# Fewer steps of the weights' sums in tile 0's output stage, their rounding copies one step behind, the second batch normalised earlier

## The chip, the core and the metric

The kernel runs on one core of one Trainium2 chip. The metric is the device time of one execution in microseconds, as the median of several executions. A core has five engines that matter here: TensorE (PE, its weight loads PEld), VectorE (DVE), ScalarE (ACT), GpSimd (POOL) and the queue that issues transfers (SP). Each takes its own instructions in the order of its queue. An instruction whose input is not there holds up all behind it on that engine.

## The reference

```python
# attention: 8 batches, 8 heads, 576 positions, 64 wide; window of 64 positions back
scores = np.matmul(q, k.transpose(0, 1, 3, 2)) / np.sqrt(64)
scores = np.where((rel >= 0) & (rel < 64), scores, -1e9)
attn = softmax(scores)                                # + 1e-9 in the sum
x = np.matmul(attn, v)  # to 4608 tokens x 512
# gated feed-forward layer, d_ff 1536
rms = np.sqrt(np.mean(x * x, axis=-1, keepdims=True) + 1e-06)
xn = x / rms * rms_g
g = xn @ w_gate
out = (g * sigmoid(g) * (xn @ w_val)) @ w_out
```

All in float32. The kernel does the large products with pairs of float16 tiles (a rounded value and the rest), three matmuls for each product.

## The kernel before, in words

The 4608 tokens are worked through in nine tiles of 512, the attention in eight batches of 576 tokens, four pairs of heads each. A tile needs the normalised output of the batches that it overlaps: tile 1 takes the last 64 tokens of batch 0 and the first 448 of batch 1. Attention of later batches runs among the matmuls of earlier tiles.

**Half-steps.** A tile has 32 half-steps: 24 of its input stage (`expert_in`: gate and value products, banks `pg` and `pv`, six blocks of 256 columns of d_ff, two accumulations of each kind in a block) and 8 of its output stage (`expert_out`: four chunks `po` of 128 tokens, 36 matmuls each; `store` drains a chunk with ScalarE into `ot`, L1219, and SP writes it out). Tile 0 spans half-steps 0 to 32, its output stage 24 to 32, tile 1 32 to 64, tile 2 64 to 96. All other work is entered in a plan with a half-step as its due time (`at_step`). Some is placed in slots, a finer count of the matmul groups (`at_slot`); `advance` issues what is due as the matmul loop passes.

**Order.** Up to the second block of tile 1 (`ORDERED = (1, 1)`) the order of the text is only a priority: a planner with its own simulated times picks what is ready for each engine. From that block on, PE, DVE, ACT and POOL keep the written order (`in_written_order`). SP's queue stays with the planner.

**Banks.** Three accumulation banks (`mo`) are shared by `pg`, `pv` and `po`; one bank (`mi`) is shared by the totals (`tot`, L756) and both broadcasts (`rb`, L835) of a batch's normalisation. Eight buffers of 2 KB (`t2k`) are shared by `th`, `ot`, `hl`, `blk` and others.

**The weights' sums.** From tile 3 on the input products use a scheme with seven products in place of eight, which needs sums of blocks of the weights. `prepare(c, step)` makes them, eight steps for each of six column blocks c: a step adds two halves of a block (`whole_block`, L1061), or combines two sums (L1096, L1101, L1104, L1109). Four of the eight steps end in `out`: ScalarE rounds the sum to float16 (`hl`, L1071), VectorE subtracts to get the rest (L1074), and two transfers write both to `sevens` in DRAM (L1076). Step 0 also writes twelve blocks of the weights as they are (L1091). `PREP` gives two windows of half-steps with a number of steps in each. `load_sevens` (L1119) reads the sums back over the old weights, at half-steps 72, 80 and 88 for the first three column blocks.

**Normalisation of batch 1.** `attention_events(1, ...)` enters scores at the eight half-steps of `S1`, transposes `LK1` later, products with the values `LV1` later, query and key loads `LQ1` earlier. The two numbers behind these are the half-steps of the two pieces: `roots` one half-step ahead of the first (squares summed into `ssq`, totals, then eleven small instructions on VectorE, L774 and L811), then for each piece a broadcast on TensorE, four scalings on VectorE (L865), four copies on ScalarE (L869) and four subtractions on POOL (L871).

**Around it.** Pairs of batch 2 are scored in visits at half-steps 24.5 and 29.5. For each, POOL then does 16 moves (L381) and VectorE three transposes (L386, L388, `turn`). The output weights are split at half-step 23 (`out_split`, L245 on ScalarE, L246 on VectorE).

Of the kernel before, what the change touches and what calls it, by code (L numbers as in the profile page):

```python
# [2 lines left out]
def E(n, d):  # L3
    return CFG.get(n, d)
# [39 lines left out]
MOVES = (8.7, 7, 4.5, 4)  # L44
FIRST7 = 3
ORDERED = (1, 1)
PREP = ((26, 32, 24), (34, 84, 25))
MASK_AT, MASK_BY, WEIGH = 1, 1, 1
MOVE_AT, MOVE_BY, TURN_AT = 11.3, 0.8, -4
NORM_AT, NORM_BY, NORM_GAP = 5, 0.75, 2  # L50
# [1 line left out]
GATE, HH_7, HH_8 = 0, 1, 1  # L52
ST = 2 * NBLK * P - D
NRB = 2
S1, LK1, LV1, LQ1 = [-2, 1, 3, 6, 10, 12.5, 15.5, 19], 2.5, 6, 7
LN2_16 = 16 * math.log(2.0)
MASKED = -3.0e38
QK_SCALE = 1.0 / math.sqrt(D)
# [4 lines left out]
def tile_window_attention_moe(  # L63
# [10 lines left out]
    nc = tc.nc  # L74
# [60 lines left out]
    for rows, cols, own in (  # L135
# [7 lines left out]
        part = mask[rows, cols]  # L143
# [487 lines left out]
    def attention_events(b, start, pace, tags):  # L631

        load_queries, load_keys, score, to_keys, values, roots, normal, moved, turned, products, drain, norm = attention(b)
        lk, lv, lq, n0, n1 = tags
        events = []
        if b < NRB:
            events = [(n0 - 1, roots), (n0, partial(normal, 0)), (n1, partial(normal, 1))]
        else:
            s0 = slot_at(visit_at(NPAIR * b + 5))
            for k, part in enumerate(normalise_all(b, norm)):  # L640
                at_slot(s0 + NORM_AT + NORM_BY * k + (NORM_GAP if k > 2 else 0), part)
        for hp in range(NPAIR):
            if b >= TB:
                n = NPAIR * b + hp
                i0 = visit_at(n) - half_steps * (b - 1)
                events.append((i0 - 7, partial(load_queries, hp)))
                events.append((i0 - 7, partial(load_keys, hp)))
                s0 = slot_at(visit_at(n))
                for k in range(16):
                    when = MOVE_AT + MOVE_BY * k if n >= RUSH else MOVE_AT - 4.7 + 0.5 * k  # L650
                    at_slot(s0 + when, partial(moved, hp, k // 4, k % 4))
                for k in range(3):
                    at_slot(slot_at(visit_at(n + 2)) + TURN_AT - 2 * (RUSH <= n < 16) + k, partial(turned, hp, k))
                visits[n] = partial(products, hp), partial(values, hp), partial(drain, hp)
                continue
            i0 = start[2 * hp]
            events.append((i0 - lq, partial(load_queries, hp)))
            events.append((i0 - lq, partial(load_keys, hp)))
            for g in range(2):
                i = start[2 * hp + g]  # L660
                events.append((i + lv, partial(values, hp, g)))
                events.append((i + lk, partial(to_keys, hp, g)))
                events.append((i, partial(score, hp, g)))
        return events
# [4 lines left out]
    def slot_at(h):  # L669

        t, r = divmod(h, half_steps)
        per = 4 * NF if t < FIRST7 else 7 * NC
        first = t * (4 * NF + NC * TT // P) - max(0, t - FIRST7) * (4 * NF - 7 * NC)
        return first + (r * per / in_phase if r < in_phase else per + (r - in_phase) * NC / 2)
# [10 lines left out]
    def at_slot(s, part):  # L685
        at_step(step_at(s) + 1e-6, part)
# [7 lines left out]
    def visit_at(n):  # L694

        n -= NPAIR * TB
        return VISITS[n] if n < 4 else VISITS[4] + 8 * (n - 4)
# [175 lines left out]
    def normalise_all(b, norm):  # L873
        return LazyParts(b, norm).parts()
# [176 lines left out]
    unfinished = []  # L1051

    def prepare(c, step):

        w = [wt[(2 * c + i) % (2 * NC)].rearrange("p a (k f) -> p a k f", k=NKD) for i in range(2)]
        s0, s1 = sums

        def whole_block(out, f, d):
            for i in range(2):
                hi, lo = (w[i][:, j, 2 * d : 2 * d + 2, f * P : (f + 1) * P] for j in range(2))  # L1060
                nc.vector.tensor_tensor(out[:, i], hi, lo, ALU.add)  # L1061

        def block(f, d):
            t = wk.tile([P, TT], F32, tag="t2k", name=f"blk_{c}_{step}", bufs=T2K)
            kept_block["b"] = t.rearrange("p (w k f) -> p w k f", w=2, k=2)
            whole_block(kept_block["b"], f, d)

        def out(src, o):
            src = src.rearrange("p w k f -> p (w k f)")
            hl = wk.tile([P, 2, TT], F16, tag="t2k", name=f"hl_{c}_{step}", bufs=T2K)  # L1070
            nc.scalar.copy(hl[:, 0], src)  # L1071

            def rest():
                nc.vector.tensor_tensor(hl[:, 1], src, hl[:, 0], ALU.subtract)  # L1074
                for j in range(2):
                    nc.sync.dma_start(  # L1076
                        out=sevens[c][:, o, :, j].rearrange("p w k f -> p w (k f)"),
                        in_=hl[:, j].rearrange("p (w n) -> p w n", w=2),
                    )

            unfinished.append(rest)

        if unfinished:
            unfinished.pop()()
        if c == NC:
            return
        if step == 0:
            for i in range(2):
                for o, k, f in ((0, 0, 0), (1, 2, 0), (6, 2, 1)):
                    for j in range(2):  # L1090
                        nc.sync.dma_start(out=sevens[c][:, o, i, j], in_=w[i][:, j, k : k + 2, f * P : (f + 1) * P])  # L1091
            whole_block(s0, 1, 0)
        elif step == 1:
            whole_block(s1, 0, 0)
        elif step == 2:
            nc.vector.tensor_tensor(s1, s1, s0, ALU.subtract)  # L1096
            out(s1, 5)
        elif step == 3:
            block(1, 1)
        elif step == 4:  # L1100
            nc.vector.scalar_tensor_tensor(s0, s0, -1.0, kept_block["b"], ALU.mult, ALU.subtract)  # L1101
            out(s0, 2)
        elif step == 5:
            nc.vector.tensor_tensor(s1, s1, kept_block["b"], ALU.subtract)  # L1104
            out(s1, 3)
        elif step == 6:
            block(0, 1)
        else:
            nc.vector.tensor_tensor(s1, s1, kept_block["b"], ALU.add)  # L1109
            out(s1, 4)  # L1110
# [153 lines left out]
    def at_step(h, part):  # L1264
        plan.append((h, len(plan), part))

    HPLACE = "8fffff"
    SEQ = E("SEQ", "00 01 02 03 04 05 o0").replace(","," ").split()
    for h, part in attention_events(1, S1, 0, (LK1, LV1, LQ1, 28, 30)):
        at_step(h, part)  # L1270
    if E("S2", None) is not None:
        for h, part in attention_events(2, E("S2", 45), E("P2", 0.8), (E("LK2", 1.5), E("LV2", 2.5), E("LQ2", 4), E("N20", 60), E("N21", 62))):
# [15 lines left out]
    rest = first_batch()  # L1288
# [12 lines left out]
    def at(name, part):  # L1301
        if name not in done0:
            at_step(DW[name], part)
# [13 lines left out]
    at("O", out_split)  # L1317
    at_step(PREP[0][0], room_for_sums)
    done = 0
    for a, z, count in PREP:  # L1320
        s0, s1 = slot_at(a), slot_at(z)
        for j in range(count):
            at_slot(s0 + (s1 - s0) * j / count, partial(prepare, *divmod(done + j, 8)))
        done += count
# [77 lines left out]
```

## Time and profile before

| | |
|---|---|
| median of 3 runs | 1033.64 us (1033.34 to 1034.03) |
| profiled execution | 1035.58 us |
| its span, first to last instruction | 1033.4 us, mean granted TensorE clock 0.977 |
| PE busy | 976.0 us, 94% |
| DVE busy | 639.3 us, 62% |
| ACT busy | 508.0 us, 49% |
| POOL busy | 505.6 us, 49% |

The output stage of tile 0 begins at 188.09 us with the first `po` matmul, and tile 1's first gate matmul starts at 230.20. In the rows of the profile a group is named by line, engine, operation and tiles (`out<-in`); behind the bar stand busy time and mean duration in ns, and idle time before it with what ended it. A timeline's row is start, duration, engine, line; in brackets the idle time before it and its releaser.

### The profile page before, as it was taken

The numbers are of one execution on the slowest core, as the hardware profiler recorded it, in microseconds if no ns is written. First come the engines' busy times: TensorE is split into PE (matmuls) and PEld (weight loads), VectorE is DVE, ScalarE is ACT, GpSimd is POOL, SyncE is SP. The second block draws the span as 40 slices with busy tenths as digits, with TensorE's granted clock in tenths as the row PEclk, the third lists the DMA queues.
The fourth block names the chain that finished last, engine by engine and source line by source line (L and its number), as shares of the span: only waits on it lengthen the run. The fifth ranks groups of instructions, "written<-read, shape, count | busy, mean of one in ns | idle before, by whom it ended". The sixth has DMA issues, their size and how long they took to land.

```text
span 1033.4 us, 20843 instructions
## 1 busy us (share of the span) xinstructions
PE 976.0 (94%) x7835; PEld 632.1 (61%) x7835; DVE 639.3 (62%) x1721; ACT 508.0 (49%) x1303; POOL 505.6 (49%) x634
## 2 busy tenths in 40 slices
PE   7788989988999999999999999999999999999998
PEld 5544434543544455478747874787478848856875
DVE  5687756796658454646775767576666655532550
ACT  5556757625444444355545554565456524522540
POOL 3334524682976467536673677467646611200210
PEclk9988988899999999999999999999999999999999
DMA  7645793224223454247624762476246515632401
GB/s 281 196 134 163 218 278 78 69 80 123 74 63 91 123 147 148 74 148 220 202 85 146 223 205 81 137 231 196 81 123 188 165 40 146 195 116 89 151 1 41
DMA packets 81316, 143.43 MB, mean 139 GB/s; under 512 B 25792, under 2 KB 38336, under 8 KB 81216
## 3 DMA queue, kind: packets, MB, share of 16 engines
q1 hardware_dynamic: 80640, 140.93, 44.8%
q8 instruction: 61, 1.00, 0.4%
q10 hardware_dynamic: 576, 1.18, 0.3%
q14 instruction: 39, 0.32, 0.1%
HBM read 121.64 MB, written 20.45 MB: 137 GB/s over the span
## 4 chain that ended last, share of the span: by engine, by line
PE 66%; DVE 18%; ACT 8%; issue 3%; DMA 3%; POOL 2%; SPq 0%; ACTq 0%; DVEq 0%; POOLq 0%
PE bk L1136 18%; PE bk L960 5%; PE bk L961 5%; PE bk L962 5%; PE xp L534 4%; PE sc L399 3%; DVE th L1176 3%; PE pv L960 3%; PE pg L962 3%; PE pg L960 3%; PE pg L961 3%; PE pv L961 3%; PE pv L962 3%; ACT th L1167 3%; DVE th L1177 3%
## 5 line engine op out<-in xcount | busy, mean ns | idle before, releaser
L1136 PEld LDWEIGHTS <-wt 128*128 128x128 f16 x3024 | 294.9, 98 | 54.7 <-issue 18.0
L381 POOL TENSOR_TENSOR pm<-pm,st 32x288 f32<-32x288 f32 (+1 forms) x384 | 274.0, 713 | 95.2 <-DVE st L449 51.6
L1136 PE MATMUL bk<-xn,wt 128*128 128x256 f16 x1728 | 209.2, 272 | 11.3 <-DVE th L1177 5.3
L981 POOL TENSOR_TENSOR h<-th,h 128x512 f16<-128x512 f32 x78 | 91.5, 1173 | 198.8 <-ACT h L981 185.3
L1136 PE MATMUL bk<-wt,wt 128*128 128x256 f16 x1224 | 150.3, 273 | 0.3 <-ACT u L1156 0.3
L960 PE MATMUL bk<-wt,h 128*128 128x512 f16 (+1 forms) x300 | 111.3, 371 | 0.0
L962 PE MATMUL bk<-wt,h 128*128 128x512 f16 (+1 forms) x300 | 111.2, 371 | 0.0
L961 PE MATMUL bk<-wt,h 128*128 128x512 f16 (+1 forms) x300 | 111.2, 371 | 0.0
L415 ACT ACTIVATE pm<-pm,st 128x128 f32<-128x128 f32 (+1 forms) x216 | 83.7, 388 | 36.9 <-DVE st L412 36.3
L1167 ACT ACTIVATE th<-bk,hsc 128x256 f32<-128x256 f32 x108 | 50.8, 471 | 99.3 <-DVE bk L1197 67.1
L981 ACT CAST h<-th 128x512 f16<-128x512 f32 x94 | 57.8, 615 | 47.8 <-DVE th L1026 33.9
L1176 DVE SCALAR_TENSOR_TENSOR th<-th,bk 128x256 f32<-128x256 f32 x108 | 45.2, 419 | 54.5 <-ACT th L1167 54.1
L960 PEld LDWEIGHTS <-h 128*128 128x128 f16 x436 | 43.2, 99 | 50.9 <-issue 7.1
L962 PEld LDWEIGHTS <-h 128*128 128x128 f16 x436 | 43.0, 99 | 49.3 <-issue 1.4
L961 PEld LDWEIGHTS <-h 128*128 128x128 f16 x436 | 43.2, 99 | 45.6 <-issue 1.3
L399 PE MATMUL sc<-kv,q 64*64 64x128 f32 (+1 forms) x1056 | 56.9, 295 | 9.4 <-DMA q<-q 5.0
L1197 DVE TENSOR_TENSOR bk<-bk,s 128x512 f32<-128x512 f32 x36 | 24.9, 693 | 57.7 <-PE bk L1136 57.7
L960 PE MATMUL pv<-xn,wt 128*128 128x512 f16 x144 | 56.1, 390 | 3.9 <-ACT wt L239 2.0
L960 PE MATMUL pg<-xn,wt 128*128 128x512 f16 x144 | 55.9, 388 | 3.7 <-ACT ot L1219 3.7
L962 PE MATMUL pg<-xn,wt 128*128 128x512 f16 x144 | 55.3, 386 | 1.3 <-DVE wt L246 1.3
L961 PE MATMUL pv<-xn,wt 128*128 128x512 f16 x144 | 55.9, 388 | 0.0
L961 PE MATMUL pg<-xn,wt 128*128 128x512 f16 x144 | 55.7, 387 | 0.0
(191 smaller groups left out, 1754.9 us busy)
## 6 DMA issues: line engine op xcount, KB each, us to landing
wt<-sevens SPq DMA_DIRECT2D x108, 512.0 KB, 4.2
kv<-kv SPq DMA_DIRECT2D x28, 608.0 KB, 4.7
wt<-sevens SPq DMA_DIRECT2D x36, 256.0 KB, 3.4
q<-q SPq DMA_DIRECT2D x28, 288.0 KB, 3.0
kv<-kv SPq DMA_DIRECT2D x56, 128.0 KB, 4.7
out<-ot SPq DMA_DIRECT2D x27, 256.0 KB, 2.0
st<-w_gate SPq DMA_DIRECT2D x6, 1024.0 KB, 6.6
st<-w_val SPq DMA_DIRECT2D x6, 1024.0 KB, 6.4
```

The costliest lines, as they stand in the source:

```text
L381: nc.gpsimd.tensor_tensor(m[to, :us, fr], p[fr, :us, to], r, ALU.mult)
L399: nc.tensor.matmul(out.rearrange("p (n c) -> p n c", c=D), lhsT=qt[hd, j * D : (j + 1) * D], rhs=halves[hd, :1, :] if j == 0 else halves[h ...
L415: nc.scalar.activation(part, part, AF.Exp, bias=low, scale=-1.0, accum_out=total)
L534: nc.tensor.matmul(xp[hd, c * D : (c + 1) * D], lhsT=vv[j][rows, hd], rhs=w, start=True, stop=True, skip_group_check=True,)
L960: nc.tensor.matmul(acc, lhsT=lh, rhs=rh, start=first, stop=False)
L961: nc.tensor.matmul(acc, lhsT=lh, rhs=rl, start=False, stop=False)
L962: nc.tensor.matmul(acc, lhsT=ll, rhs=rh, start=False, stop=last)
L981: part()
L1136: nc.tensor.matmul(acc[:, i * HT : (i + 1) * HT], lhsT=w[:, i, l, kt, :], rhs=b[:, m, kt, :], start=at_start, stop=kt == 1 and j == 2, ski ...
L1167: nc.scalar.activation(cols, acc[:, :HT], AF.Tanh, scale=th_scale[:, c : c + 1])
L1176: nc.vector.scalar_tensor_tensor(cols, cols, 1.0, acc[:, :HT], ALU.add, ALU.mult)
L1177: nc.vector.scalar_tensor_tensor(cols, acc[:, HT:], 2.0**-41, cols, ALU.mult, ALU.mult)
```

## The change

The first window of the weights' sums holds 9 steps from half-step 27.5 instead of 24 from 26; the second holds 41 from 35 to 88 instead of 25 from 34 to 84. A sum's rounding copy is issued at the next call of `prepare`, its subtraction and transfers at the call after that; before, the copy was issued at once and the rest at the next call. One more call empties the list. Batch 1's values are entered 5 instead of 6 half-steps after the scores, and the last pair's two scores at 15 and 18 instead of 15.5 and 19. Its normalisation is entered at 24.5 and 27 instead of 28 and 30.

```diff
-PREP = ((26, 32, 24), (34, 84, 25))
+PREP = ((27.5, 32, 9), (35, 88, 41))
...
-S1, LK1, LV1, LQ1 = [-2, 1, 3, 6, 10, 12.5, 15.5, 19], 2.5, 6, 7
+S1, LK1, LV1, LQ1 = [-2, 1, 3, 6, 10, 12.5, 15, 18], 2.5, 5, 7
...
             hl = wk.tile([P, 2, TT], F16, tag="t2k", name=f"hl_{c}_{step}", bufs=T2K)
-            nc.scalar.copy(hl[:, 0], src)
 
             def rest():
...
-            unfinished.append(rest)
-
-        if unfinished:
-            unfinished.pop()()
+            unfinished.append([partial(nc.scalar.copy, hl[:, 0], src), rest])
+
+        for parts in unfinished:
+            parts.pop(0)()
+        unfinished[:] = [parts for parts in unfinished if parts]
         if c == NC:
             return
...
-    for h, part in attention_events(1, S1, 0, (LK1, LV1, LQ1, 28, 30)):
+    for h, part in attention_events(1, S1, 0, (LK1, LV1, LQ1, 24.5, 27)):
```

## The prediction

> **What bounds the kernel now.** I read the page's slices first, then the waits of TensorE, then the queues of the engines that it waits for.
>
> ```profile
> PE   7788989988999999999999999999999999999998
> PEclk9988988899999999999999999999999999999999
> ```
>
> A digit is 25.8 us. From the eleventh digit on TensorE is full. What can be won lies ahead of that, in the first 250 us, or after it only in crumbs. The table by stage (columns: busy us of PE, PEld, DVE, ACT and POOL, then granted clock) compares the part of tile 0's output stage where the weights' sums run, all of tiles 1 and 2, and in these the stretch where VectorE is fullest:
>
> ```profile
> 206.50:243.00 36.50, 28.38 (x189) 14.09 (x188) 34.63 (x56) 11.77 (x24) 23.49 (x25) 0.95 0.34 98
> 245.00:440.00 195.00, 195.00 (x1344) 95.97 (x1343) 115.66 (x329) 88.60 (x251) 127.74 (x159) 1.00 0.34 101
> 310.00:337.00 27.00, 27.00 (x137) 12.88 (x136) 22.13 (x61) 11.75 (x35) 17.39 (x23) 1.00 0.29 87
> ```
>
> In the first row VectorE works 34.63 of 36.50 us and TensorE has holes. In the second it is the other way round: TensorE has none, VectorE works 59%. The waits of TensorE from 188 to 246 us (waiter, releaser: total, times, longest):
>
> ```profile
> PE pg L960 <- ACT ot L1219: 3.7, 1, 3.7
> PE rb L835 <- DVE xb L865: 3.5, 1, 3.5
> PE po L960 <- ACT wt L245: 2.3, 1, 2.3
> PE pv L960 <- ACT ot L1219: 0.9, 1, 0.9
> ```
>
> TensorE also runs slowly after the two long ones. Its timeline, matmuls of 128x512 each (start, duration; the fifth and sixth row are full speed, ten matmuls between them):
>
> ```profile
> 222.04 0.60 PE L960 MATMUL po<-wt,h 128*128 128x512 f16 x1
> 225.42 0.41 PE L962 MATMUL po<-wt,h 128*128 128x512 f16 x1
> 242.78 0.58 PE L960 MATMUL pg<-xn,wt 128*128 128x512 f16 x1 [3.69 <-ACT ot L1219]
> 245.72 0.50 PE L961 MATMUL pg<-xn,wt 128*128 128x512 f16 x1
> 226.32 0.38 PE L960 MATMUL po<-wt,h 128*128 128x512 f16 x1
> 228.69 0.38 PE L962 MATMUL po<-wt,h 128*128 128x512 f16 x1
> ```
>
> Full speed is 2.37 / 11 = 0.215 us a matmul. From 222.04 to 225.42 there are 8 steps: 3.38 - 8 x 0.215 = 1.65 us lost. From 242.78 to 245.72 there are 7: 2.94 - 1.51 = 1.43 us lost. Who holds TensorE up is read in the other queues:
>
> ```profile
> 241.52 0.62 ACT L1071 CAST hl<-sum 128x512 f16<-128x512 f32 x1 [2.16 <-DVE sum L1109]
> 242.05 0.68 ACT L1219 ACTIVATE ot<-po,hsc 128x512 f32<-128x512 f32 x1
> 206.57 1.30 DVE L386 STREAM_TRANSPOSE pm<-pm 128x512 f32<-128x512 f32 x2 [4.53 <-POOL pm L381]
> 218.12 2.44 DVE L865 SCALAR_TENSOR_TENSOR xb<-xb,gsb,rb 128x448 f32<-128x448 f32 x4
> 189.55 31.14 POOL L381 TENSOR_TENSOR pm<-pm,st 32x288 f32<-32x288 f32 x32 [5.90 <-ACT pm L415]
> ```
>
> ScalarE takes its queue in order. The last drain of tile 0 (ot at 242.05), which frees the bank that the next gate accumulation needs, stands behind a rounding copy (L1071) which waited for VectorE's sum. The normalisation of the second batch (L865 at 218.12) stands behind seven steps' sums; the second broadcast (rb) needs the bank that these four instructions read, so TensorE waits for them.
>
> **The change part by part.** (1) Fifteen of the 24 steps leave the output stage; nine stay. Their VectorE work, first the instructions that touch the sums (window, busy), then the blocks' additions, each for the two windows:
>
> ```profile
> 206.50:243.00 36.50, 24.35 (x33) 0.95 0.34 98
> 245.00:440.00 195.00, 24.61 (x34) 1.00 0.34 101
> L1061 DVE TENSOR_TENSOR blk<-wt 128x256 f32<-128x256 f16 x12 | 6.3, 561 | 0.0
> L1061 DVE TENSOR_TENSOR blk<-wt 128x256 f32<-128x256 f16 x12 | 8.0, 703 | 0.0
> ```
>
> Steps 3 to 23 lie in the first window: 24.35 + 6.3 = 30.7 us, 1.46 each. Fifteen make 21.9 us, which leaves VectorE 12.7 of 36.5 us. Steps 24 to 48 lie in the second: 24.61 + 8.0 = 32.6 us, 1.30 each. Fifteen more add 19.5 us to 115.66, or 69% of the 195 us. TensorE is the cover there; I take 0 us, with the price if cover fails in the rivals.
>
> (2) The copies (0.62 us on ScalarE) go a step behind the sum and the subtractions two steps behind. Four copies are left in the output stage instead of twelve, and a copy finds its sum a step old. So drains no longer queue behind a sum in the making: the waits 3.7 and 0.9 go, and 1.43 us of slow matmuls with the first. VectorE's turn at 206.57 still waits for POOL, so the first copies may still wait; next late would be the second drain, but its bank is first needed by tile 1. The rounded pair's buffer is held one step longer, of eight shared ones: nothing, unless a later copy waits for one. The fiftieth step is an empty call. In tiles 1 and 2 a step comes each 53/41 = 1.29 half-steps on average instead of 50/25 = 2.
>
> (3) Normalisation at 24.5 and 27 instead of 28 and 30, the roots at 23.5 instead of 27. L865 then stands ahead of the sums, and the wait of 3.5 and its 1.65 us go. The cost is that the first broadcast comes close behind the roots. These rows are the first and the last of the roots' chain on VectorE, the broadcast's place now, and the wait of batch 0, whose broadcast stands right behind its roots:
>
> ```profile
> 192.09 0.15 DVE L774 TENSOR_SCALAR rm<-tot 128x5 f32<-128x5 f32 x1
> 200.27 0.57 DVE L811 SCALAR_TENSOR_TENSOR rm<-rm 128x5 f32<-128x5 f32 x1
> 209.49 1.00 PE L835 MATMUL rb<-ident,rm 128*128 128x128 f32 x8
> PE rb L835 <- DVE rm L811: 4.2, 1, 4.2
> ```
>
> The chain takes 200.84 - 192.09 = 8.75 us, and the broadcast, 8.65 us after it, waits for nothing now. A wait here is between 0 (this row) and 4.2 us (batch 0, which had no other matmuls to put between; here stand 4 x 36 po matmuls by the code). I take 2.0. On POOL four subtractions come after L865,
>
> ```profile
> 220.77 5.15 POOL L871 TENSOR_TENSOR xn<-xb,xn 128x448 f16<-128x448 f32 x4
> ```
>
> and they are now written ahead of the moves, so the turn that waits for the moves can be 5 us later; VectorE's 22 us of new slack hide that.
>
> (4) Batch 1's last scores, transposes and values are written 0.5 to 2 half-steps earlier in tile 0. This adds nothing, but may move ScalarE's copy and square ahead of the split that TensorE waits 2.3 us for. I take 0, between a gain priced below and a loss of the same size.
>
> (5) Transfers. The twelve direct ones of each sixth of the weights are in SP's queue early whatever their step:
>
> ```profile
> L1091 SPq DMA_DIRECT2D sevens<-wt x72: 359/462/1513, 49.4 to 162.2; - x72
> SPq L1076 <- ACT hl L1071: 41.9, 12, 11.8
> 250.52 0.76 DVE L1061 TENSOR_TENSOR sum<-wt 128x256 f32<-128x256 f16 x2
> ```
>
> All 72 went out by 162.2 us, so moving step 16 moves none for certain. Of the written pairs eight move, with 16 transfers. SP's queue holds them until copy and subtraction are done (11.8 us at worst so far), with the loads of keys and queries behind; those are written 7 half-steps ahead. DMA is at 0.34 there. I take 0. The first reload reads only sums of the nine early steps and the one after them, and the last reading of old weights is written at about half-step 82, ahead of their reload at 88.
>
> Sum: 3.7 + 3.5 + 0.9 + 1.65 + 1.43 = 11.2 us gained, 2.0 lost: -9.2. The profiled execution took 1035.58 us (span 1033.4), 1.94 over the median of 1033.64. It would be 1026.4, and the median 1024.4.
>
> **The rivals.** Broadcast waits like batch 0's: 4.2 and then 1.65 of slow matmuls instead of 2.0, so 11.2 - 5.85 = 5.35 gained: **1028.3**. For it speaks the same order of events in batch 0, against it the po matmuls to fill with. Chance 0.13.
>
> The wait at 188 goes too. After it the matmuls were slow as well:
>
> ```profile
> 191.50 0.59 PE L961 MATMUL po<-wt,h 128*128 128x512 f16 x1
> 194.44 0.54 PE L962 MATMUL po<-wt,h 128*128 128x512 f16 x1
> ```
>
> Seven steps in 2.94 us, 1.43 too many: 2.3 + 1.43 = 3.7 more, **1020.7**. Chance 0.12.
>
> The added steps crowd tiles 1 and 2, **1033.4**. They are additions and subtractions of two tiles, which take longer beside POOL's moves (shortest/median/longest ns):
>
> ```profile
> L1061 DVE TENSOR_TENSOR sum<-wt x24: 366/420/1248, 184.5 to 350.9; 128x256 f32<-128x256 f16 x24
> L1074 DVE TENSOR_TENSOR hl<-sum,hl x24: 639/690/1158, 209.7 to 395.5; 128x512 f16<-128x512 f32 x24
> L1024 ACT ACTIVATE th<-pg,hsc 128x512 f32<-128x512 f32 x23 | 15.7, 683 | 14.4 <-PE pg L962 14.4
> L1025 DVE SCALAR_TENSOR_TENSOR th<-th,pg 128x512 f32<-128x512 f32 x23 | 15.8, 689 | 42.3 <-ACT th L1024 42.2
> ```
>
> A gate's bank is needed again two accumulations later, 24 x 0.215 = 5.2 us; tanh and scaling take 0.68 + 0.69, which leaves 3.8 us. A subtraction and a block at their longest are 1.16 + 2 x 1.25 = 3.7: just inside. Were each of the 15 added steps to overrun by 0.6, behind masks or turns, 9 us of the 9.2 would be given back. Against it: the scaling waited 42.3 us for its input, so VectorE is mostly early, and TensorE did not wait once from 245 to 440 us, not even where VectorE had 22.13 of 27. Chance 0.07. [...]
>
> The steps come forward anyway: up to the second block of tile 1 a planner orders the instructions, and could fill VectorE with later steps as before: **1033.6**. Against it: step 24 ran at 250.52, where it is written, not earlier. Chance 0.04.
>
> Slower: the planner puts the broadcast straight behind the totals.
>
> ```profile
> 188.09 1.44 PE L960 MATMUL po<-wt,h 128*128 128x512 f16 x3 [2.27 <-ACT wt L245]
> 189.35 2.29 PE L756 MATMUL tot<-one,ssq 128*128 128x1 f32 x10
> ```
>
> TensorE then waits the chain out, 200.84 - 191.64 = 9.2, is slow after it (1.65), and the second broadcast still waits for L865 (3.5 + 1.65): 16.0 lost against 11.2 gained, **1038.4**. It decides from 11.2 us of such waits on. The totals' early place, 1.26 us after the stage's first po matmul at 188.09, speaks for it; the broadcast's place now, 20 us behind them with all its inputs 8 us old, shows at least that it need not come first. Chance 0.07.
>
> **How the numbers follow.** My own case has the rest, 0.57, and by itself spans 1021.5 to 1027.5 (no broadcast wait and some crumbs; or 3 us of crowding). The range of 1019.5 to 1030.0 takes in the two neighbours: 0.57 + 0.13 + 0.12 = 0.82. A change under 0.2% (2.1 us) can't be told from none. Faster: 0.57 + 0.13 + 0.12 = 0.82; same: 0.07 + 0.04 = 0.11; slower: 0.07.
>
> **What would show it.** Right: between tile 0's first po matmul and tile 1's second gate accumulation no wait for ot or xb; L865 ahead of most sums; VectorE near a third busy in the late part of that stage; tile 1's first gate matmul some 3 us and its second gate accumulation some 8 us earlier, 9 once the slow matmuls are past; from there to the end the same distances. Wrong: rb waiting for rm for over 4 us; th waits of TensorE between 235 and 430 us; VectorE still full up to tile 1; or tile 0's input stage ending later than at 184 us, which would mean that the attention written earlier displaced something there.

## The result, and the profile after

The changed kernel takes **1025.58 us** (median of 6 runs, 1022.7 to 1029.22) against 1033.84 us (6 runs, 1033.04 to 1035.79) for the kernel before: a ratio of 0.992 (95% interval 0.990 to 0.9941), or 8.3 us less. Run again beside other kernels it gave 1026.0 us, ratio 0.9937 (0.9915 to 0.9959). The forecast was 1024.4 us. The profiled execution is the longest of the six, 1029.22 us with a span of 1027.4; the sums below are taken between executions profiled in the same way, and every verdict rests on the timed medians.

The slices of the page, 25.7 us a digit (25.8 before): the low digits, but for the last one, all lie in the first 206 us.

```profile
PE   7788979799999999999999999999999999999998
```

The table by stage of the changed kernel, in the two windows shown of before (busy us of PE, PEld, DVE, ACT, POOL; granted clock):

```profile
206.50:243.00 36.50, 36.50 (x211) 17.34 (x209) 14.51 (x29) 10.77 (x22) 13.58 (x18) 0.98 0.26 84
245.00:440.00 195.00, 193.15 (x1359) 95.56 (x1358) 143.81 (x356) 91.24 (x254) 137.07 (x163) 1.00 0.37 108
```

VectorE fell from 34.63 to 14.51 of 36.5 us and TensorE has no hole left there. But in tiles 1 and 2 VectorE rose by 28.2 us, to 74% of the stretch, and TensorE is no longer whole: 193.15 of 195. The waits of TensorE from 178 to 250 us and, last row, from 245 to 440:

```profile
PE rb L835 <- DVE rm L811: 4.2, 1, 4.2
PE sc L399 <- DVE st L412: 1.8, 1, 1.8
PE sc L399 <- DMA kv<-kv: 1.2, 1, 1.2
...
PE xp L534 <- DVE pm L388: 1.8, 2, 1.4
```

All four waits shown of before are gone: `ot` 3.7 and 0.9, `xb` 3.5, `wt` 2.3. The drains come off the matmuls directly, as ScalarE's timeline shows (none stands behind a rounding copy that waits for a sum):

```profile
206.56 0.69 ACT L1219 ACTIVATE ot<-po,hsc 128x512 f32<-128x512 f32 x1 [0.84 <-PE po L962]
214.57 0.68 ACT L1219 ACTIVATE ot<-po,hsc 128x512 f32<-128x512 f32 x1
222.06 0.69 ACT L1219 ACTIVATE ot<-po,hsc 128x512 f32<-128x512 f32 x1 [6.30 <-PE po L962]
229.87 0.69 ACT L1219 ACTIVATE ot<-po,hsc 128x512 f32<-128x512 f32 x1 [3.33 <-PE po L962]
```

In their place stands a new wait: the first broadcast of the second batch waits 4.2 us for the roots. VectorE's timeline shows why:

```profile
196.98 0.17 DVE L811 TENSOR_TENSOR rm<-rm 128x5 f32<-128x5 f32 x1
201.01 1.30 DVE L386 STREAM_TRANSPOSE pm<-pm 128x512 f32<-128x512 f32 x2 [3.87 <-POOL pm L381]
202.24 0.22 DVE L811 SCALAR_TENSOR_TENSOR rm<-rm 128x5 f32<-128x5 f32 x1
202.38 0.30 DVE L388 STREAM_TRANSPOSE pm<-pm 64x128 f32<-64x128 f32 x1
202.61 0.57 DVE L811 SCALAR_TENSOR_TENSOR rm<-rm 128x5 f32<-128x5 f32 x1
204.44 2.46 DVE L865 SCALAR_TENSOR_TENSOR xb<-xb,gsb,rb 128x448 f32<-128x448 f32 x4 [1.26 <-PE rb L835]
```

The chain of the roots has two short steps to go at 197.1 us. Between them and the rest the planner has put a turn (L386, L388) of batch 2, which waits 3.87 us for POOL's moves. VectorE sits idle with 0.8 us of work in hand that TensorE needs. TensorE waits, and is slow afterwards, as its timeline shows (the last row is full speed again):

```profile
203.32 1.07 PE L835 MATMUL rb<-ident,rm 128*128 128x128 f32 x8 [4.21 <-DVE rm L811]
204.24 0.58 PE L961 MATMUL po<-wt,h 128*128 128x512 f16 x1
207.60 0.43 PE L961 MATMUL po<-wt,h 128*128 128x512 f16 x1
207.86 0.38 PE L962 MATMUL po<-wt,h 128*128 128x512 f16 x1
```

Between 204.24 and 207.60 lie eight steps: 3.36 - 8 x 0.215 = 1.64 us lost. The broadcast's wait therefore costs 4.2 + 1.64 = 5.85 us.

Where the time went, stage by stage, from the start times in the timelines of several profiles (us; "output" runs from tile 0's first `po` matmul to tile 1's first gate matmul, "tile 1" from there to the first `po` matmul of tile 1; kernels not met yet are those of the next section):

| kernel | first `po` | output | tile 1 | span |
|---|---|---|---|---|
| before | 188.1 | 42.1 | 78.9 | 1033.4 |
| changed | 185.4 | 44.2 | 74.0 | 1027.4 |
| changed, run again | 182.2 | 44.0 | 74.0 | 1024.1 |
| sums_only | 183.8 | 36.6 | 74.0 | 1018.3 |
| norm_back | 183.4 | 37.6 | 74.0 | 1018.8 |
| norm_15 | 183.0 | 37.7 | 72.6 | 1017.5 |
| turn_behind | 184.4 | 38.5 | 74.0 | 1020.8 |
| sums_back | 180.1 | 44.3 | 72.3 | 1021.1 |
| copy_only | 188.1 | 40.4 | 79.7 | 1032.5 |
| attn_only | 180.3 | 42.3 | 77.9 | 1025.1 |
| copy_attn | 186.5 | 37.8 | 79.2 | 1028.0 |

What follows, from tile 1's first `po` matmul to the end, takes 723.8 to 724.6 us in all of them. The first `po` matmul of tile 0 is not quite the same point of the work in all rows: with the attention entered earlier, the ten matmuls of the totals (`tot`) stand ahead of it and 22 score matmuls of a visit behind it; in before, sums_only and copy_only it is the other way round. Two readings: the output stage itself did not become shorter by the change (42.1 to 44.2), since the broadcast's wait, and the score matmuls with their wait for keys, took the place of what went; and the first column varies by several us between runs of the same kernel (185.4 and 182.2), so single spans do not settle differences of that size.

### The profile page after: what moved, and what is told of

Its sections match the earlier page's. It is cut to its first block, busy times and chain, and to the rows that moved or that the text cites. A ratio compares the mean times of both kernels' runs of the same rounds, so it can differ in the third digit from the quotient of the medians.

```text
span 1027.4 us, 20830 instructions
## 1 busy us (share of the span) xinstructions
PE 971.2 (95%) x7835; PEld 630.7 (61%) x7835; DVE 646.3 (63%) x1721; ACT 508.0 (49%) x1303; POOL 508.8 (50%) x634
## 4 chain that ended last, share of the span: by engine, by line
PE 68%; DVE 17%; ACT 7%; issue 3%; DMA 2%; POOL 2%; SPq 0%; DVEq 0%; ACTq 0%; POOLq 0%
PE bk L1136 18%; PE bk L960 5%; PE bk L961 5%; PE bk L962 5%; PE xp L534 4%; PE sc L399 4%; DVE th L1176 3%; ACT th L1167 3%; PE po L962 3%; PE po L961 3%; PE po L960 3%; DVE th L1177 3%; PE pg L962 3%; PE pg L960 3%; PE pv L960 3%
## 5 line engine op out<-in xcount | busy, mean ns | idle before, releaser
L381 POOL TENSOR_TENSOR pm<-pm,st 32x288 f32<-32x288 f32 (+1 forms) x384 | 276.8, 721 | 92.8 <-DVE st L449 53.3
L399 PEld LDWEIGHTS sc<-kv,q 64*64 64x64 f32 x1056 | 43.7, 146 | 22.8 <-issue 12.2
L960 PE MATMUL pg<-xn,wt 128*128 128x512 f16 x144 | 55.4, 384 | 0.2 <-ACT wt L245 0.2
L961 PE MATMUL pg<-xn,wt 128*128 128x512 f16 x144 | 55.3, 384 | 0.0
```

Source lines behind the costliest of these rows:

```text
L381: nc.gpsimd.tensor_tensor(m[to, :us, fr], p[fr, :us, to], r, ALU.mult)
L399: nc.tensor.matmul(out.rearrange("p (n c) -> p n c", c=D), lhsT=qt[hd, j * D : (j + 1) * D], rhs=halves[hd, :1, :] if j == 0 else halves[h ...
L960: nc.tensor.matmul(acc, lhsT=lh, rhs=rh, start=first, stop=False)
L961: nc.tensor.matmul(acc, lhsT=lh, rhs=rl, start=False, stop=False)
```

## The experiments

The kernels ran in three groups, each on one chip beside the kernel before, whose medians there were 1032.9 us (after_again, norm_back, turn_behind, sums_back), 1033.33 (sums_only, copy_only, copy_back, attn_only) and 1034.5 (norm_mid, copy_attn, norm_15).

**The changed kernel again, as the base of its group** (after_again).

> The changed kernel once more, for its spread and a second profile. If the wait of the first broadcast of batch 1 (rb on rm) lies in the order of the queues, the profile shows it again at 4 us with slow matmuls behind it, at any total from 1023 to 1029 us. If it came from the slow transfer of that one execution, it is under 1 us in a faster one.

1026.0 us (1025.22 to 1029.98). TensorE's wait for the roots is in this profile too, 4.4 us: it belongs to the kernel and not to one execution.

**The normalisation put back** (norm_back).

```diff
-    for h, part in attention_events(1, S1, 0, (LK1, LV1, LQ1, 24.5, 27)):
+    for h, part in attention_events(1, S1, 0, (LK1, LV1, LQ1, 28, 30)):
```

> The changed kernel with the normalisation of batch 1 at 28 and 30 again; the sums' windows, late copies and earlier attention stay. Theory 1a (with the sums gone from VectorE the scalings come in time from 28 on too, and at 24.5 the broadcast only waits): the wait of 4.2 and the 1.6 us of slow matmuls behind it go, 1020 to 1023 us. Theory 1b (the scalings must come early, or the second broadcast waits for them as before): 1028 to 1030 us.

**1019.48 us** (1018.96 to 1020.64), ratio to before 0.9869 (0.9846 to 0.9893): 6.5 us less than the changed kernel beside it. Waits of TensorE, 178 to 250 us, and the broadcast's matmuls (count, shortest/median/longest ns, first and last start):

```profile
PE sc L399 <- DVE st L412: 1.8, 1, 1.8
PE sc L399 <- DMA kv<-kv: 1.0, 1, 1.0
PE xp L534 <- DVE pm L388: 0.3, 1, 0.3
```

```profile
L835 PE MATMUL rb<-ident,rm x12: 219/275/275, 204.4 to 213.1; 128*128 128x128 f32 x6, 128*128 128x64 f32 x6
```

VectorE's queue in this kernel:

```profile
194.73 0.17 DVE L811 TENSOR_TENSOR rm<-rm 128x5 f32<-128x5 f32 x1
198.76 1.30 DVE L386 STREAM_TRANSPOSE pm<-pm 128x512 f32<-128x512 f32 x2 [3.87 <-POOL pm L381]
200.36 0.60 DVE L811 SCALAR_TENSOR_TENSOR rm<-rm 128x5 f32<-128x5 f32 x1
```

The turn still splits the roots, with the same wait for POOL. But the broadcast stands 3.5 us behind the last root (204.4 against 200.96) and waits for nothing, and there is no wait for `xb` either. With the sums out of the stage, the normalisation did not need to come earlier.

**The turn held back** (turn_behind). The changed kernel with one order more: the transposes of the turn (pair 8) are issued on VectorE only behind the fourth scaling of the second batch.

```diff
+            if b == 1 and piece == 0 and kt == 3:
+                scaled_at["last"] = next(
+                    x for x in reversed(nc.cur_bb.bb.instructions) if x.engine == nc.vector.engine
+                )
...
-            turn(p, m, part)
+            with ExitStack() as order:
+                if b * NPAIR + hp == 8:
+                    order.enter_context(tc.issue_after(scaled_at["last"]))
+                turn(p, m, part)
```

> The changed kernel with one order added: VectorE's transposes of pair 8 are issued behind the first four scalings of batch 1, so that the roots' last two steps no longer stand behind transposes which wait 3.87 us for POOL's moves. Theory 3 (the broadcast waits because of that): the wait for rm falls from 4.2 to under 1 us, the slow matmuls behind it go, 5 us less than the changed kernel, about 1020 us. Theory 4 (the roots' chain among the splits is late by itself): the wait stays at 3 to 4 us and the time within 1 us of the changed kernel's.

1022.22 us (1020.33 to 1023.01), 0.989 (0.9866 to 0.9915): 3.8 us less than the changed kernel beside it. Lines of this kernel are shifted by 1 to 4: L815, L869 and L839 are the roots, scalings and broadcast. VectorE's timeline, then TensorE's wait for the broadcast:

```profile
196.43 0.67 DVE L815 SCALAR_TENSOR_TENSOR rm<-rm 128x5 f32<-128x5 f32 x2
198.36 2.46 DVE L869 SCALAR_TENSOR_TENSOR xb<-xb,gsb,rb 128x448 f32<-128x448 f32 x4 [1.26 <-PE rb L839]
200.73 1.30 DVE L387 STREAM_TRANSPOSE pm<-pm 128x512 f32<-128x512 f32 x2
```

```profile
PE rb L839 <- DVE rm L815: 1.5, 1, 1.5
```

The chain runs through and the transposes, behind the scalings, no longer wait for POOL. The wait falls from 4.2 to 1.5 us, not to under 1, the rest being that the broadcast stands right behind the chain. The turn inside the chain is shown as the cause of the larger part of the loss. It is the attention entered earlier that puts the turn there: in every profile of a kernel with it but this one, L386 stands ahead of the last two root instructions (attn_only: 196.15 us, against 197.38 and 197.75), and in before, sums_only and copy_only it stands behind the last one (before: 206.57 against 200.27).

**The normalisation half way** (norm_mid).

```diff
-    for h, part in attention_events(1, S1, 0, (LK1, LV1, LQ1, 24.5, 27)):
+    for h, part in attention_events(1, S1, 0, (LK1, LV1, LQ1, 26, 28.5)):
```

> The changed kernel with the normalisation between the two places, at 26 and 28.5. Theory 3 (the broadcast's distance from the roots' end in TensorE's queue is what counts; the roots end after the transposes that wait for POOL): the wait for rm falls from 4.2 to 0 to 2 us, 1020 to 1023 us. If the planner puts the broadcast where its inputs are ready by its own times whatever the half-step, the wait and the time stay as in the changed kernel.

1025.56 us (1023.91 to 1029.06), 0.9913 (0.9898 to 0.9929): as the changed kernel. TensorE waits 4.6 us for the roots. The broadcast hardly moved with its half-step from 24.5 to 26 (18.4 us behind the first `po` matmul, 17.9 in the changed kernel), so the second theory is the one that holds: the planner placed it by its own times. At 28 (norm_back) it stands 21.0 us behind; where between 26 and 28 this changes was not tried.

**The sums put back into the stage** (sums_back), with the rest of the change left in.

```diff
-PREP = ((27.5, 32, 9), (35, 88, 41))
+PREP = ((26, 32, 24), (34, 86, 26))
```

> The changed kernel with the two windows of the weights' sums as before (24 steps from 26 to 32, the rest from 34 to 86 at 2 half-steps each); late copies, earlier attention and earlier normalisation stay. Theory 1 (the fifteen steps on VectorE in the output stage held the drains and scalings up): back to 1031 to 1034 us, VectorE over 90% busy there, waits of TensorE for ot again. Theory 2 (the gain comes from the attention of batch 1 entered earlier, which lets tile 0's input stage end 4.7 us sooner): at most 1.5 us over the changed kernel.

1025.33 us (1023.32 to 1028.63), 0.9925 (0.9903 to 0.9947): the same as the changed kernel and not theory 1's 1031 to 1034, although VectorE is full again (32.93 us of the 36 from 200 to 236). The number is theory 2's, but its reason falls short: the earlier attention alone brings 3.4 us (attn_only, below). ScalarE's timeline, then TensorE's wait for the broadcast:

```profile
227.77 1.22 ACT L1083 CAST hl<-sum 128x512 f16<-128x512 f32 x2 [1.41 <-DVE sum L1101]
228.89 0.68 ACT L1219 ACTIVATE ot<-po,hsc 128x512 f32<-128x512 f32 x1
```

```profile
PE rb L835 <- DVE rm L811: 4.2, 1, 4.2
```

The last drain stands behind copies that waited for a sum, as in the kernel before, and yet TensorE does not wait for it. The reading is that the 4.2 us at the broadcast delay TensorE by as much as the drains are late; copy_attn below, which differs only in the normalisation's place, bears it out. Shown is that in the presence of the early normalisation moving the 15 steps brings nothing.

**The sums moved alone** (sums_only): the kernel before with the changed `PREP` only.

```diff
-PREP = ((26, 32, 24), (34, 84, 25))
+PREP = ((27.5, 32, 9), (35, 88, 41))
```

> The kernel before with the two windows of the weights' sums alone (9 steps from 27.5, 41 from 35 to 88), copies at once. Theory 1: nearly the whole gain, 9 to 11 us under the kernel before, no wait for ot or xb. Theory 5 (the copies' order is what counts; few copies are left here, so the drains are free either way): the same waits gone, so both theories allow it; together with copy_only it says whether either edit alone would do. If the waits for ot stay at 2 us or more, the sums' place is not the cause at all.

1023.22 us (1020.06 to 1024.44), 0.9904 (0.9886 to 0.9923): 10.1 us less than before, by the medians more than the whole change brings (8.3 and 6.9). Its waits of TensorE from 178 to 250 us are one row:

```profile
PE po L960 <- ACT wt L245: 2.3, 1, 2.3
```

The waits for `ot` and `xb` go with the sums, with copies issued at once and the normalisation at 28.

**The late copies alone** (copy_only): the kernel before with the changed `prepare`, one step more in the second window for the call that empties the list.

```diff
-PREP = ((26, 32, 24), (34, 84, 25))
+PREP = ((26, 32, 24), (34, 86, 26))
...
-            nc.scalar.copy(hl[:, 0], src)
...
-            unfinished.append(rest)
+            unfinished.append([partial(nc.scalar.copy, hl[:, 0], src), rest])
...
```

> The kernel before with the late copies alone (24 steps from 26 to 32, the rest from 34 to 86). Theory 5 (the drains waited because ScalarE's copies stood in front of them waiting for sums, not because VectorE was full): the waits for ot of 3.7 and 0.9 and the slow matmuls behind go, the wait for xb of 3.5 stays with its slow matmuls, 5 to 7 us under the kernel before. Theory 1 (VectorE full): within 2 us of the kernel before.

1031.93 us (1031.45 to 1037.62), 0.9992 (0.9975 to 1.0008): no difference that can be told. Waits of TensorE, then ScalarE's timeline (`hl` is the rounding copy, L1083 here):

```profile
PE pg L960 <- ACT ot L1219: 5.0, 1, 5.0
PE rb L835 <- DVE xb L865: 3.1, 1, 3.1
PE po L960 <- ACT wt L245: 2.3, 1, 2.3
```

```profile
218.24 0.62 ACT L1083 CAST hl<-sum 128x512 f16<-128x512 f32 x1 [5.04 <-DVE sum L1109]
...
237.82 1.22 ACT L1083 CAST hl<-sum 128x512 f16<-128x512 f32 x2 [1.40 <-DVE sum L1101]
238.94 0.68 ACT L1219 ACTIVATE ot<-po,hsc 128x512 f32<-128x512 f32 x1
```

A copy written a step later still waits in front of the drain, and its releaser is still VectorE's sum, as long as 24 steps crowd the stage. The last drain does start 3.1 us earlier than before (238.94 against 242.05 us), but the matmuls of a visit that TensorE had done ahead of the waiting gate accumulation (from 236.54 to 239.1 us in before) now stand behind it (from 244.18), so the wait there is longer, and at tile 1's first `po` matmul only 0.9 us of lead is left (308.21 against 309.07).

**The copies put back** (copy_back), with the rest of the change left in (`prepare` as before).

> The changed kernel with the copies at once again; nine steps, earlier attention and normalisation stay. Theory 5a (with nine steps it does not matter when a sum is copied): within 1 us of the changed kernel. Theory 5b (the copies must be late): waits for ot of 2 to 4 us come back and the time is 2 to 5 us over the changed kernel's.

1027.14 us (1025.42 to 1030.64), 0.9949 (0.993 to 0.9969); the changed kernel's intervals, 0.9915 to 0.9959 and 0.990 to 0.9941, overlap it. No wait for `ot` comes back. With nine steps in the stage the late copies are worth 1.1 to 1.6 us by the medians, 1.2 to 3 us by the ratios, and not told from nothing.

**The attention written earlier, alone** (attn_only).

```diff
-S1, LK1, LV1, LQ1 = [-2, 1, 3, 6, 10, 12.5, 15.5, 19], 2.5, 6, 7
+S1, LK1, LV1, LQ1 = [-2, 1, 3, 6, 10, 12.5, 15, 18], 2.5, 5, 7
```

> The kernel before with the attention of batch 1 entered earlier alone (last scores at 15 and 18, values 5 behind). Theory 2 (tile 0's input stage ends sooner by it): the first po matmul at 180 to 185 us instead of 188, and 3 to 5 us under the kernel before, with the output stage's waits as before. Against it: within 1.5 us of the kernel before.

1029.92 us (1026.93 to 1032.69), 0.9966 (0.9951 to 0.9982): 3.4 us less than before. Its waits of TensorE from 178 us:

```profile
PE pg L960 <- ACT ot L1219: 3.9, 1, 3.9
PE rb L835 <- DVE xb L865: 1.8, 1, 1.8
PE sc L399 <- DMA kv<-kv: 1.7, 1, 1.7
```

The wait for `wt` at 188 us is gone, that for `xb` is 1.7 us shorter, and one for keys (1.7) is new. Taking off TensorE's wait for the first weights (1.2 to 5.3 us over the profiles), the first `po` matmul starts at 177.7 to 183.5 us in the ten profiles with the early attention and at 182.6 to 185.1 us in the three without it (means 180.0 and 184.2). That does not place the gain, since the order of the work around this matmul differs (see the table above), and with it a wait for keys or weights of 0.4 to 1.7 us that now stands behind it. Which of the small waits it takes away was not separated.

**Late copies and early attention, 24 steps in the stage, normalisation at 28** (copy_attn): what the early normalisation is worth there.

```diff
-PREP = ((27.5, 32, 9), (35, 88, 41))
+PREP = ((26, 32, 24), (34, 86, 26))
...
-    for h, part in attention_events(1, S1, 0, (LK1, LV1, LQ1, 24.5, 27)):
+    for h, part in attention_events(1, S1, 0, (LK1, LV1, LQ1, 28, 30)):
```

> The changed kernel with the sums' windows and the normalisation as before; late copies and earlier attention stay. Beside sums_back it tells what the earlier normalisation is worth while 24 steps are still in the output stage. Theory 6 (it puts the scalings ahead of the sums, which is worth 4 to 6 us there, and costs the broadcast's wait, which is hidden because VectorE would have been late by as much): 1028 to 1030 us, the waits for ot and xb there, so 3 to 5 us over sums_back. Theory 7 (the late copies are what freed the drains in sums_back): 1025 us or less, no wait for ot.

1027.25 us (1025.66 to 1030.27), 0.9936 (0.992 to 0.9952). TensorE waits 4.8 us for `ot` and 1.7 for `xb`. The same kernel with the normalisation at 24.5 is sums_back, 0.9925 (0.9903 to 0.9947): with full windows the early normalisation costs nothing, and if anything gains 1 us, less than either theory had. Counted from the first `po` matmul, the last drain ends at much the same place in both (48.6 us here, 49.4 in sums_back), while tile 1's first gate matmul comes at 37.8 us here and at 44.3 there: in sums_back TensorE is late, not the drain early. With nine steps the early normalisation costs 6.5. The two edits, fewer sums in the stage and the normalisation ahead of them, are answers to the same waits, and only the second has a price of its own. Against attn_only, 0.9966 (0.9951 to 0.9982), this kernel adds the late copies alone: 3 us by the ratios, with intervals that just touch, so what they are worth beside the early attention stays open.

**Fifteen steps instead of nine in the stage, normalisation at 28** (norm_15).

```diff
-PREP = ((27.5, 32, 9), (35, 88, 41))
+PREP = ((27.5, 32, 15), (35, 88, 35))
```

> norm_back with 15 steps from 27.5 in the output stage and 35 from 35 to 88, instead of 9 and 41. If the added steps in tile 1 cost its wait for the transposes of pair 9 (1.4 us, and 1.7 us from tile 1's first gate matmul to its first output matmul against sums_back), a part of that goes and the time is 0 to 1.5 us under norm_back. If six more steps in the output stage hold the last drain up again, it is 1 to 4 us over it, with waits for ot.

1019.65 us (1017.81 to 1021.35), 0.986 (0.9843 to 0.9877): the same as norm_back. Its table by stage:

```profile
206.50:243.00 36.50, 36.50 (x213) 17.44 (x212) 30.61 (x63) 17.11 (x44) 16.51 (x19) 1.00 0.35 107
245.00:440.00 195.00, 193.67 (x1423) 98.68 (x1422) 126.95 (x336) 90.14 (x250) 130.07 (x161) 1.00 0.37 110
```

VectorE is at 30.61 of 36.5 us in the first window and TensorE still has no hole there. The waits of `xp` for the turn in tile 1 fall from 1.8 us in norm_back (two, the longer 1.4) to one of 0.6, and tile 1 takes 72.6 us instead of 74.0. In the time this is within the spread. These two versions beat both kernels, by 1.3 to 1.4% and by some 0.6%.

## Why the prediction was right, and where its terms were not

The time came out 1.2 us above the forecast, inside the range and inside the own case's range. It is right in sum because two misses cancel (the early normalisation cost far more than its charge, the early attention brought 3.4 us that were put at nothing), which is luck; the working was not right in each step.

- **Step 1, the sums, the mechanism: right.** VectorE's sums in the output stage held the drains and the scalings; alone, their move brings 10.1 us, where steps 2 and 3 had credited the same waits and slow stretches (11.2 us) to the whole change. That the added steps cost nothing in tiles 1 and 2: missed, by a little. They added 28.2 us of VectorE, not 19.5, and TensorE's `xp` there waits 1.8 us for turns whose transposes have sums between them. Against sums_back tile 1 is 1.7 us longer. The crowding rival came in at a fifth of its price; it is no wait for `th`, as the prediction looked for.
- **Step 2, the late copies: the waits go, but not by them.** Alone they bring the last drain forward by 3.1 us and the time by nothing that can be told, and without them the waits do not return.
- **Step 3, the early normalisation: the step that failed.** Credited with 3.5 + 1.65 gained and charged 2.0 for the broadcast's wait. The gain belonged to the sums, since norm_back has no wait for `xb`. The charge was 4.2 + 1.64 = 5.85, to the digit that of the first rival ("broadcast waits like batch 0's"). The reason given for 2.0, po matmuls to fill with, does not help when the planner places the broadcast by its own times, as norm_mid shows. The chain's 8.75 us was read off the trace; that the turn, which in the kernel before came after the chain and waited 4.53 us for POOL, would fall into it once the attention moved ahead was not seen.
- **Step 4, the early attention: priced 0, worth 3.4.** The second rival ("the wait at 188 goes too", 3.7 us) came true by this step. In the changed kernel a wait of 1.8 and one of 1.2 for other things stand near by, so the gain is not simply that wait, and where it comes from stays open. The rival's 1.43 us was also read too small: it counts the slow matmuls from 191.50 us on, but the granted clock of the kernel before is 0.50 from 188 us, and the three `po` matmuls at 188.09 (1.44 us) were slow as well.
- **Step 5, transfers: right as far as seen.** No wait of TensorE for weights or sums appeared in tiles 1 and 2.

The account from the parts, by medians within each group: -10.1 (sums) - 3.4 (attention) + 6.5 (normalisation) = -7.0 us, against -6.9 and -8.3 us measured of the whole; whatever the copies bring lies in what remains. The parts were measured beside different kernels and need not add up: norm_back's -13.4 fits the first two (-13.5), but copy_attn's -7.3 is more than its copies (-1.4) and its attention (-3.4) make alone.

Of the signs listed: no wait for `ot` or `xb`, right. L865 ahead of the sums, right. VectorE at 14.51 of 36.5, 40%, near the third. Tile 1's first gate matmul came 0.6 us earlier instead of 3, because of the broadcast; its second gate accumulation came 8.0 us earlier (234.80 against 242.78), as listed, but a visit's 2.5 us of matmuls that stood ahead of it now come behind it, so that agreement is in part luck. At tile 1's first `po` matmul the lead was 5.4 us in this execution, and the distance from there to the end changed by 0.6. Tile 0's last value matmul started at 175.97 us (180.65 before), so the input stage did not end late. "rb waiting for rm for over 4 us" was listed as the sign of error, and it is what the profile shows.

On what the added steps and POOL's moves did to each other: rows by form in 245 to 440 us, first of before, then of the changed kernel (busy us, mean ns):

```profile
L1074 DVE TENSOR_TENSOR hl<-sum,hl 128x512 f16<-128x512 f32 x12 | 9.4, 782 | 0.0
L381 POOL TENSOR_TENSOR pm<-pm,st 32x288 f32<-32x288 f32 x64 | 48.5, 758 | 18.7 <-DVE st L449 10.8 <-DVE pm L388 2.5 <-PE pv L962 1.8
```

```profile
L1073 DVE TENSOR_TENSOR hl<-sum,hl 128x512 f16<-128x512 f32 x20 | 19.1, 954 | 0.0
L381 POOL TENSOR_TENSOR pm<-pm,st 32x288 f32<-32x288 f32 x64 | 52.3, 817 | 18.3 <-DVE st L449 7.4 <-ACT h L981 4.5 <-PE pv L962 1.5
```

The same subtraction takes 954 instead of 782 ns and the same POOL move 817 instead of 758: both engines' instructions grew longer with more of the steps in this stretch. That VectorE's take longer beside POOL's moves, as the crowding rival says, the trace of before shows: three subtractions (L1074) that run while POOL moves (189.55 to 220.69 us) take 1.10 to 1.16 us, and two while POOL stands idle (234.42 to 245.71 us) 0.69 each. The rise is not put down to the number of steps alone: POOL's move takes 789 ns in sums_only (the same steps, copies at once) and 766 in norm_15 (35 steps, late copies), and what the late copies add was not separated. POOL's busy time rose by 9.3 us, with four more instructions. The turn, which needs both engines, is where TensorE pays: 1.8 us.

## What to carry to other kernels

When two edits answer the same wait, price each with the other in place: here the second one had nothing left to gain and kept its cost, so leaving it out was worth 6.5 us. A wait that has been hidden is judged by what stands between producer and consumer in each in-order queue: look for an instruction there that waits for a third engine, because it puts that engine's lateness into the chain (here the turn's 3.87 us for POOL; with the turn behind the scalings TensorE's wait fell from 4.2 to 1.5 us). A copy issued later helps a queue only as far as its input is by then in time: while the producer was full here, it brought the last drain 3.1 us forward, and the time did not follow.

## What the runs showed of the hardware

- The slow matmuls also came without a long wait ahead of them, after 1.82 us at most. Stretches of the changed kernel at the start of the output stage (busy us of PE, PEld, DVE, ACT and POOL, then granted clock):

```profile
180.00:184.00 4.00, 1.95 (x28) 1.60 (x24) 3.96 (x23) 3.73 (x18) 0.00 (x0) 0.97 0.25 76
184.00:187.00 3.00, 2.87 (x11) 1.68 (x10) 2.95 (x10) 3.00 (x9) 2.77 (x3) 0.50 0.86 248
187.00:190.00 3.00, 1.89 (x23) 1.38 (x24) 2.97 (x8) 2.44 (x4) 2.83 (x4) 0.50 0.49 145
190.00:194.00 4.00, 4.00 (x11) 1.44 (x10) 4.00 (x5) 2.10 (x2) 3.82 (x4) 0.50 0.00 0
194.00:197.00 3.00, 3.00 (x15) 1.36 (x14) 2.97 (x5) 0.19 (x1) 2.88 (x3) 0.99 0.00 0
```

  The clock is at half from 184 to 194 us, and the `po` matmuls of this stretch come every 0.43 us instead of 0.215. The waits of TensorE ahead of 184 us are 1.82 us (up to 182.19) and 0.23; the wait of 1.24 us for keys (up to 188.11) lies inside the slow stretch and did not begin it. Some 4 us are lost in it, an estimate: half of the 10 us without the wait. After the broadcast the slow stretch, 3.36 us from 204.24 us on, follows a wait of 4.2 us; at 184 us the longest wait ahead was 1.82, and from the end of the wait for keys it took 5.9 us of work until the full rate was back. What sets the start and the length of such a stretch no run here shows.
- The time of one kernel varied by several us between executions. Between the two profiles of the changed kernel, 3.2 of the 3.3 us lie ahead of the output stage, and TensorE's wait for the first weights was 1.2 to 5.3 us over all profiles. The mean granted clock goes along with the time: of attn_only's twelve executions, the four with a clock of 0.982 or more have spans of 1025.5 to 1026.9 us and the seven with 0.977 or 0.978 of 1027.9 to 1030.9; whether it is cause or consequence no run separates. Differences of 1 to 2 us, such as that of the late copies, could not be settled with 4 to 12 runs each.
